# Softmax attention on one core: the loop head of TensorE moved to another fetch slot, a blank score fill ahead of the data, held-back first loads and a shallower VectorE

## The chip, the cores and the metric

The kernel runs on one core of one Trainium2 chip. The metric is the device time of one execution in microseconds (us); medians are over the runs of one kernel, and a ratio compares kernels that ran on the same chip in the same job. A job compares each kernel with fresh runs of the kernel before. The jobs of the experiments ran on different chips: the kernel before had 824.22 us in the first job, 823.03 in that of e0 to e3, 825.05 for e4 to e8, 825.07 for e9 to e11 and 824.69 for e12. So where a median is set beside that of "the control" (e0_again) across jobs, a difference below 2 us shows nothing. "Ratio" below is the mean time of one kernel's fast runs over that of the other kernel's fast runs of the same rounds, so it is not quite the ratio of the medians that stand beside it.

A profile is one execution with the hardware's records. Its span is about 1.7 us shorter than the time of the same execution. Times inside a profile count from the start of its span.

## The reference

```python
B, H, Sq, Sk, D = 16, 32, 192, 1024, 128      # all bf16
scores = jnp.einsum("bhqd,bhkd->bhqk", q, k) * D ** -0.5
p = softmax(scores, axis=-1)
out = jnp.einsum("bhqk,bhkd->bhqd", p, v)
```

512 heads are worked on in 128 tiles of four heads. One tile loads 1 MB of K, 1 MB of V and 192 KB of Q and stores 192 KB.

## The kernel before

Each tile is worked in three *fills*. A fill is one batch of score matmuls (48 or 64 of them, 32 rows each) into PSUM; ScalarE exponentiates it; VectorE turns K and Q for later fills, GpSimd puts K (`order`) and V (`spread`) in the layout that TensorE wants. Four fills later the matching *PV round* of 32 matmuls multiplies with V, and VectorE normalises it (`onorm`). There are 384 fills. TensorE runs them in a hardware loop of 64 turns, six fills (two tiles) a turn; the other engines are unrolled. TensorE's program:

```python
for _i in range(12):                       # warm-up, on a tile of ones
    pe.matmul(o_ps..., ones[:], ones...)
pe.wait_ge(s_set, 3)                       # buffers of the first, empty PV rounds are set
with nc.Fori(0, NF // (3 * R), engines=[PE], head_slot={PE: 100}):
    pv(-1 - LAG, (1,))                     # second half of the round that the turn before left open
    for f in range(3 * R):
        qk(f)                              # scores of fill f
        pv(f - LAG, (0,) if f == 3 * R - 1 else (0, 1))
pv(NF - 1 - LAG, (1,))
for s in range(NF - LAG, NF): pv(s)        # [tail, cut]
```

`head_slot` fixes the place (0 to 255) of the loop's first instruction in a block of 256 instructions. In the built program the loop has 1050 instructions: 512 matmuls of two instructions each and 26 others. SyncE issues the loads without a wait until buffers run out, and VectorE turns K five fills ahead of the fill it stands at:

```python
load_k(0); load_k(1); load_q(e, 1)
for n in range(2, NKN):                    # NKN = 5 buffers
    load_v(n - 2); load_k(n); load_q(e, n)
# VectorE, in order:
for f in range(NF + LAG + 1):
    if f - 5 >= 0: onorm(f - 5)            # [range check of the sums near the end, cut]
    g = f + 5
    if g < NF: turn_k(g)                   # ahead of it turn_q(x) for the third piece of a tile
```

VectorE takes this program in its order: while it waits for a K load in `turn_k`, it can't normalise, and TensorE can't begin the next PV round, because the program has one PSUM buffer for them.

## Time and profile before

| reading | before |
|---|---|
| median time, 4 runs | 824.22 us (823.38 to 825.35) |
| span of the profile, granted clock | 823.1 us, 0.996 |
| first real scores (fill 0) start | 8.62 us |
| fill 8 starts | 36.12 us |
| fill 383, the last, starts | 812.92 us |

In the steady part three fills take 6.21 us, or 2.07 us a fill. The table by stretches shows TensorE full there. Its columns are the stretch, its length, busy time and instructions of each engine, the granted clock of TensorE, the share and the rate of the DMA engines. The kernel before:

```profile
0.00:25.00 25.00, 15.93 (x428) 11.54 (x428) 12.15 (x14) 11.91 (x10) 14.39 (x19) 0.93 0.94 364
600.00:800.00 200.00, 200.00 (x8260) 178.38 (x8250) 149.77 (x322) 187.13 (x194) 137.49 (x163) 1.00 1.01 388
```

So TensorE bounds the steady part, and only the head leaves room. The timeline of TensorE in the head of the kernel before follows. Its columns are start, length, engine, line, operation, tiles, shape, count, and in brackets the idle time before it with what ended it. L628 is a score fill, L650 a PV round. "issue" means that no wait which the profile shows explains the idle time.

```profile
12.79 0.29 PE L628 MATMUL f_s<-f_qt,f_kt 32*128 32x128 bf16 x8
15.49 0.98 PE L628 MATMUL f_s<-f_qt,f_kt 32*128 32x128 bf16 x40 [2.41 <-issue]
16.41 1.10 PE L650 MATMUL f_o<-f_vp,f_pt 128*64 128x129 bf16 x32
17.44 1.09 PE L628 MATMUL f_s<-f_qt,f_kt 32*128 32x192 bf16 x48
18.46 0.36 PE L650 MATMUL f_o<-f_vp,f_pt 128*64 128x129 bf16 x6
21.87 1.62 PE L650 MATMUL f_o<-f_vp,f_pt 128*64 128x129 bf16 x26 [3.06 <-issue]
23.43 1.73 PE L628 MATMUL f_s<-f_qt,f_kt 32*128 32x192 bf16 x64
...
28.46 1.89 PE L628 MATMUL f_s<-f_qt,f_kt 32*128 32x128 bf16 x46 [2.12 <-issue]
```

Three stops stand in the middle of fills or rounds, 126 and 124 matmuls apart: about 250 instructions and the semaphore instructions between them, one block. After the second stop 64 score matmuls take 1.73 us instead of 1.10: the trace records the clock at 0.5 there, from 21.43 to 24.84 us (called cold below). The packets of the queues tell the rest; the page counts them by queue:

```profile
q14 instruction: 32, 0.26, 0.1%
q8 instruction: 5, 0.08, 0.0%
```

### The profile page before, as it was taken

How to read it: one execution, taken by the hardware profiler on the slowest of the kernel's cores; microseconds unless marked ns; L12 is line 12 of the kernel's file. 1: busy time of each engine (PE TensorE's matmuls, PEld its weight loads, DVE VectorE, ACT ScalarE, POOL GpSimd, SP SyncE). 2: the span in 40 equal slices, each digit the busy share in tenths (PEclk: the TensorE clock that was granted, in tenths of full speed). 3: DMA queues.
4: the chain of work that ended last, by engine and by line, in shares of the span. 5: the costliest groups of instructions: out<-in, count | busy, mean ns of one | idle time of the engine just before them, and what ended most of it. 6: DMA issues, size and time to landing. Idle time of an engine off the chain costs nothing. (4 is left out here: it accounts for less than half of the span.)

```text
span 823.1 us, 71558 instructions
## 1 busy us (share of the span) xinstructions
PE 807.8 (98%) x32926; PEld 717.7 (87%) x32926; DVE 599.6 (73%) x1288; ACT 748.5 (91%) x770; POOL 549.6 (67%) x646
## 2 busy tenths in 40 slices
PE   6899999999999999999999999999999999999998
PEld 4788888888888888888888888888888888888887
DVE  5477777777777777777777777777777777777775
ACT  5699999999999999999999999999999999999996
POOL 6466676676676666767667667667666666766762
PEclk9899999999999999999999999999999999999999
DMA  9999999999999999999999999999999999999961
GB/s 355 401 403 406 407 403 407 403 402 404 405 401 394 405 402 402 402 401 391 406 403 399 404 404 394 404 405 397 400 407 395 403 400 402 401 405 401 399 226 59
DMA packets 138293, 319.14 MB, mean 388 GB/s; under 512 B 7184, under 2 KB 56336, under 8 KB 121872
## 3 DMA queue, kind: packets, MB, share of 16 engines
q1 hardware_dynamic: 105376, 294.22, 91.3%
q10 hardware_dynamic: 32880, 24.58, 8.9%
q14 instruction: 32, 0.26, 0.1%
q8 instruction: 5, 0.08, 0.0%
HBM read 293.60 MB, written 25.17 MB: 387 GB/s over the span
## 5 line engine op out<-in xcount | busy, mean ns | idle before, releaser
L801 ACT ACTIVATE f_pt<-f_s 128x1536 bf16<-128x1536 f32 x384 | 554.9, 1445 | 3.2 <-PE f_o L650 3.2
L583 POOL COPY f_kt<-f_kx 128x768 uint32<-128x768 uint32 (+1 forms) x384 | 293.5, 784 | 254.4 <-DVE f_kx L712 134.2
L628 PE MATMUL f_s<-f_qt,f_kt 32*128 32x192 bf16 (+2 forms) x20480 | 422.9, 226 | 6.9 <-issue 4.5
L650 PE MATMUL f_o<-f_vp,f_pt 128*64 128x129 bf16 x12336 | 424.7, 222 | 3.3 <-issue 3.3
L650 PEld LDWEIGHTS f_o<-f_vp,f_pt 128*64 128x64 bf16 x12336 | 365.2, 110 | 54.3 <-issue 24.8
L628 PEld LDWEIGHTS f_s<-f_qt,f_kt 32*128 32x128 bf16 x20480 | 348.2, 92 | 43.2 <-issue 7.4
L712 DVE STREAM_TRANSPOSE f_kx<-f_kn 128x768 uint32<-128x768 uint32 (+1 forms) x384 | 334.1, 871 | 8.7 <-DMA f_kn<-in_k_dram 8.7
L798 ACT ACTIVATE f_pt<-f_s 128x512 bf16<-128x512 f32 x384 | 229.2, 597 | 63.1 <-PE f_s L628 32.9
L592 POOL COPY f_vp<-f_vs 128x1024 uint32<-128x1024 uint32 x256 | 259.1, 1040 | 8.4 <-PE f_o L650 8.4
L733 DVE RECIPROCAL f_rinv<-f_o 128x2 f32<-128x2 f32 x381 | 64.8, 170 | 195.9 <-PE f_o L650 195.9
L737 DVE TENSOR_TENSOR f_ob<-f_o,f_rinv 128x256 bf16<-128x256 f32 x381 | 161.6, 424 | 13.3 <-DVE f_rinv L733 0.3
L721 DVE STREAM_TRANSPOSE f_qt<-f_qn 128x384 uint32<-128x384 uint32 x128 | 72.8, 569 | 0.0
L675 PE MATMUL f_o<-f_ones 128*128 128x512 bf16 x12 | 4.4, 540 | 1.1 <-POOL f_ones L574 1.1
L675 PEld LDWEIGHTS f_o<-f_ones 128*128 128x128 bf16 x12 | 1.5, 131 | 3.5 <-issue 2.2
L575 POOL MEMSET f_vp<- 128x4352 uint32 x1 | 3.7, 3728 | 0.0
L695 DVE MEMSET f_pt<- 128x3072 uint32 x1 | 2.6, 2618 | 1.5 <-PEq L829 1.5
L650 PE MATMUL f_s<-f_vp,f_pt 128*64 128x129 bf16 x96 | 3.1, 220 | 0.4 <-PEq L611 0.4
L650 PEld LDWEIGHTS f_s<-f_vp,f_pt 128*64 128x64 bf16 x96 | 2.8, 110 | 0.5 <-issue 0.5
L788 ACT ACTIVATE f_pt<-f_ones 128x3072 f32<-128x3072 bf16 x1 | 2.8, 2762 | 0.0
L788 ACT ACT_TABLE_LOAD x1 | 1.3, 1283 | 1.2 <-PEq L829 1.2
L733 DVE RECIPROCAL f_rinv<-f_s 128x2 f32<-128x2 f32 x3 | 0.5, 171 | 1.4 <-PE f_s L650 1.4
L689 PE MATMUL f_o<-f_bad,f_ones 128*1 128x1 bf16 x1 | 0.2, 164 | 1.3 <-DVEq L779 1.3
(13 smaller groups left out, 5.3 us busy)
## 6 DMA issues: line engine op xcount, KB each, us to landing
f_kn<-in_k_dram SPq DMA_DIRECT2D x128, 1024.0 KB, 10.6
f_vs<-in_v_dram SPq DMA_DIRECT2D x128, 1024.0 KB, 8.4
f_qn<-in_q_dram SPq DMA_DIRECT2D x127, 192.0 KB, 10.5
out_dram<-f_ob ACTq DMA_DIRECT2D x62, 384.0 KB, 9.5
out_dram<-f_ob SPq DMA_DIRECT2D x1, 384.0 KB, 3.2
out_dram<-f_ob SPq DMA_DIRECT2D x2, 192.0 KB, 2.3
f_qn<-in_q_dram ACTq DMA_DIRECT2D x1, 192.0 KB, 5.0
```

Source lines behind the costliest of these rows:

```text
L583: gp.tensor_copy(kt[:, x % NKT].bitcast(U32).rearrange("p U (j s u) c -> p U j s (u c)", s=2, u=2)[:, lo:hi], kx[:, x % 2].rearrange("p (U ...
L592: gp.tensor_copy(vp[:, x % NVP, 2 * T * i: 2 * T * i + 2 * T, 0:D].bitcast(U32), vs[:, x % NVS, 2 * i: 2 * i + 2, :].rearrange("p a (t d) ...
L628: ins = pe.matmul(S[:, c0: c0 + n1 - n0], kt[r, x % NKT, 2 * t + h, :, c], qt[r, x % R, h, n0:n1, c], start=w == 0 and g == 0, stop=w == 3 ...
L650: return pe.matmul(O[m0: m0 + m, u, 0:129], pt[:, x % R, 2 * y + z, t * SQ + n0: t * SQ + n0 + m], vp[:, x % NVP, (2 * y + z) * T + t, 0:129],
L675: pe.matmul(o_ps[:].rearrange("p a b -> p (a b)"), ones[:], ones[:].unsqueeze(1).to_broadcast([128, 4, 128]), start=True, stop=True)
L712: dve.transpose(kx[:, x % 2].rearrange("p (U s j u) -> p s u U j", s=2, j=32, u=2)[:, :, :, lo:hi], kn[:, x % NKN].rearrange("p (s u U i) ...
L721: dve.transpose(qt[:, x % R].bitcast(U32).rearrange("p b (y j u) c -> p u y b (j c)", y=3, u=2), qn[:, x % NKN].rearrange("p (u y b i) -> ...
L733: dve.reciprocal(ri, O[:, :, 128]).then_inc(s_rc, 1)
L737: dve.tensor_tensor(ob[:, so, 6 * a + 2 * w: 6 * a + 2 * w + 2, :], O[:, :, 0:128], ri.unsqueeze(2).to_broadcast([128, 2, D]), ALU.mult,). ...
L788: act.activation(pt[:, 1].rearrange("p a c -> p (a c)").bitcast(F32), ones[:, 0:1].to_broadcast([128, 2 * T * SQ]), ACT_FN.Copy).then_inc( ...
L798: act.activation(pt[:, x % R, 0, c], s1_ps[:], ACT_FN.Exp, scale=scale).then_inc(s_e1, 1)
L801: act.activation(pt[:, x % R, 1:4, c], s3_ps[f % 2][:], ACT_FN.Exp, scale=scale).then_inc(s_e3, 1)
```

## The change

The intent: have the first blocks of the loop fetched while TensorE waits for K0 anyway, keep the loads out of the way of the later ones, and let VectorE not stand in front of loads that now come later. Cut to its core:

```diff
-    BLANK = LAG + 1
+    PRE = 1                                   # one blank score fill ahead of the data
+    BLANK = LAG + 1 + PRE
+    AHEAD = 3
 # SyncE
                 for n in range(2, NKN):
+                    if n == 2: e.wait_ge(s_qk, PRE + 1)      # scores of fill 0 done
                     load_v(n - 2)
+                    if n == 2: e.wait_ge(s_pv, BLANK - 2)    # PV round of fill 1 done
                     load_k(n)
                     load_q(e, n)
 # TensorE
-                for _i in range(12):          # warm-up
+                for _i in range(2):
-                             head_slot={mybir.EngineType.PE: 100}):
-                    pv(-1 - LAG, (1,))
-                    for f in range(3 * R):
+                             head_slot={mybir.EngineType.PE: 226}):
+                    pv(-PRE - 1 - LAG, (CLOSE, 32))
+                    for f in range(-PRE, 3 * R - PRE):
                         qk(f)
-                        pv(f - LAG, (0,) if f == 3 * R - 1 else (0, 1))
+                        pv(f - LAG, (0, CLOSE if f == 3 * R - PRE - 1 else 32))
+                for f in range(NF - PRE, NF): # the last fill stands behind the loop now
+                    qk(f); pv(f - LAG)
 # VectorE
-                    g = f + 5
-                    if g < NF:
+                    g = f + AHEAD
+                    if 5 <= g < NF:
```

Cut away: smaller, earlier memsets (so that the loop can be entered near 2.3 us instead of 5.7), zeros in the K and Q buffers that the blank fill reads, and all semaphore counts raised by PRE. The number of matmuls in a turn is the same.

## The prediction

> **What bounds the kernel now.** In the table by stretches, TensorE is busy 200.0 of 200 us from 200 to 800 us. The timeline gives a steady fill (one score fill plus one PV round) every 2.07 us: 812.92 - 34.01 us over 376 fills. 384 such fills are 795 us; the rest of the 823.1 us span is a head and a tail. The change leaves the matmuls of a fill and the tail alone, so only the head can pay.

> **The head.** In the timeline the first real scores start at 8.62 us, after K0 has landed (6.4 us). Fill 7 starts at 34.01 us; at 2.07 us a fill it would start at 23.1. So 10.9 us are lost. TensorE stops three times with releaser "issue", no semaphore: 2.41 us (ends 15.49), 3.06 (21.87), 2.12 (28.46). After the last two, matmuls run slow for a while (48 to 64 in 1.73 to 1.89 us instead of 1.10). Ahead of each stop's end the trace has one 16 KB packet of the second instruction queue (13.03, 19.35, 25.91 us). [...] The stops lie about 126 matmuls apart: two instructions each plus semaphore instructions, 256. So a block takes 5.5 to 6.6 us from entering the previous one, behind loads moving at 400 GB/s, and TensorE eats it in 3.1.

> **What the change does.** The loop is 1050 instructions (512 matmuls, 26 others). With its head at slot 226 the first crossing comes after 15 matmuls, near 2.5 us instead of 9.9; the blank fill runs while TensorE would wait for K0. So block 2 should be there when needed (about 9.5 us). Block 3 is requested near 9.5 us, with K1 landed and V0 only just issued, needed near 12.4; block 4 near 13, ahead of K2. With a quiet queue I estimate 4 us a fetch (the tail's packet at 817.9 us plus the 1.5 us seen from landing to resumption), so two stops of about 1 us each remain. The added fill is free under the wait for K0; with fewer warm-up matmuls TensorE may meet fill 0 cold (up to 1.2 us). Delayed loads: K2 lands near 18.5 us instead of 15.6, for fill 6 at 21 us or later; V0 near 14.5 for a round at 18. With VectorE three fills ahead, it no longer blocks the normalisations long behind K2 and K3; I allow 0.5 us. In steady state the later turning leaves the V spread about 0.5 us before its round: tight, no loss expected.

> **Sum.** 10.9 gained, less about 2 (stops), 0.7 (clock), 0.5 (data): 7.7 us, so about 817.2 us; range 814.0 to 821.0. Faster by over 2% 0.02, within 2% 0.97, slower 0.01.

> **What would show it.** Right: TensorE's "issue" stops in the waits shrink from 7.6 us to under 3; the first fetch packet lies before 9 us; fill 7 starts at 25 to 27.5 us; later fills every 2.07 us; about 10 us from the last score fill to the end, as before.

> **What would prove it wrong.** Fetches still taking 6 us with few loads in flight; VectorE waiting for K2 or K3 so long that TensorE stops instead; a stop each turn behind the V spread (period over 2.07 us, worth 128 times its length); a fetch stop on leaving the loop, since the code after it is longer by 80 matmuls.

The times at which it has blocks requested rest on the inference above, that a block is requested when TensorE enters the one before it; the traces show packets, not requests.

## The result

| | before | after |
|---|---|---|
| median | 824.22 us (4 runs) | 819.27 us (4 runs, 818.63 to 821.35) |
| ratio | | 0.9943 (95%: 0.9919 to 0.9967) |
| span of the profile, clock | 823.1 us, 0.996 | 816.9 us, 1.000 |
| fill 0 / fill 8 / fill 383 start | 8.62 / 36.12 / 812.92 us | 8.89 / 28.39 / 806.71 us |
| fill 383 to the end of the span | 10.18 us | 10.19 us |

The gain is 4.95 us by the medians, 6.2 us between the two profiles; the changed kernel's profile is of the fastest of its four runs. Fill 7 starts 8.99 us sooner (25.02 against 34.01), fill 8 starts 7.73 us sooner, fill 383 only 6.21 us sooner: 1.52 us of the head's gain are lost again on the way, and this is not the end after the last fill, which is unchanged.

The timeline of TensorE in the head of the changed kernel (L646 is a score fill, L673 a PV round):

```profile
12.04 0.90 PE L673 MATMUL f_o<-f_vp,f_pt 128*64 128x129 bf16 x25
13.41 0.41 PE L673 MATMUL f_o<-f_vp,f_pt 128*64 128x129 bf16 x7 [0.47 <-issue]
...
17.27 0.34 PE L646 MATMUL f_s<-f_qt,f_kt 32*128 32x128 bf16 x10 [0.50 <-issue]
...
25.02 1.11 PE L646 MATMUL f_s<-f_qt,f_kt 32*128 32x192 bf16 x64
27.36 1.10 PE L673 MATMUL f_o<-f_vp,f_pt 128*64 128x129 bf16 x32 [1.23 <-PEq L629]
28.39 1.10 PE L646 MATMUL f_s<-f_qt,f_kt 32*128 32x128 bf16 x48
```

The two fetch stops that are left are half a microsecond each, and no matmul after them is slow. The fetch packets start at 7.07, 10.68, 14.83 and 21.17 us. From one resumption to the next (13.41 to 17.27) are 3.9 us, against 6.4 and 6.6 before. By the issues and landings in the traces, one load of 1 MB (V0) was under way at 13.41 us; at 15.49 us in the kernel before there were seven. A third stop of 1.23 us ends with "PEq": by the profile TensorE's sequencer waited for a semaphore. It is the wait for a normalisation; VectorE stood in front of K3, which landed at 25.7 us.

The waits of VectorE for K show this, first before, then after (columns: who waited for whom, us in total, times, longest):

```profile
DVE f_kx L712 <- DMA f_kn<-in_k_dram: 8.7, 3, 3.6
```

```profile
DVE f_kx L736 <- DMA f_kn<-in_k_dram: 15.3, 11, 6.3
```

The table by stretches of the changed kernel shows what the held-back loads cost: 290 GB/s in the first 25 us instead of 364. Its clock of 1.00, against 0.93, leaves out the start: the clock records of this profile begin at 7.43 us, and the blank fill ahead of that was slow (48 matmuls in 1.89 us), at no cost, since TensorE waited for K0 afterwards.

```profile
0.00:25.00 25.00, 20.85 (x690) 17.23 (x690) 11.94 (x22) 18.02 (x18) 14.60 (x21) 1.00 0.83 290
600.00:800.00 200.00, 199.97 (x8237) 178.15 (x8235) 149.38 (x323) 186.98 (x194) 137.33 (x161) 1.00 1.02 390
```

And the loads stay late for the whole run. The list of DMA issues gives the median time from issue to landing; the kernel before, then the changed one:

```profile
f_kn<-in_k_dram SPq DMA_DIRECT2D x128, 1024.0 KB, 10.6
f_vs<-in_v_dram SPq DMA_DIRECT2D x128, 1024.0 KB, 8.4
```

```profile
f_kn<-in_k_dram SPq DMA_DIRECT2D x128, 1024.0 KB, 18.1
f_vs<-in_v_dram SPq DMA_DIRECT2D x128, 1024.0 KB, 16.3
```

Near the end TensorE stops once more, for 0.64 us, in the PV round behind fill 382. The timeline of the changed kernel there:

```profile
803.94 1.10 PE L646 MATMUL f_s<-f_qt,f_kt 32*128 32x192 bf16 x64
805.68 1.10 PE L673 MATMUL f_o<-f_vp,f_pt 128*64 128x129 bf16 x32 [0.64 <-PEq L629]
806.71 1.09 PE L646 MATMUL f_s<-f_qt,f_kt 32*128 32x128 bf16 x48
```

**Theory.** The head gains because the fetches come early and meet few loads. What is lost again has three sources: (a) the loads, held back, run without a lead for the rest of the run, so late ones stop TensorE; (b) with VectorE three fills ahead the range check stands in front of the last turns; (c) the clock: the four runs have clocks 1.0, 1.0, 0.998, 0.995 and spans 816.9, 817.0, 818.0, 819.6 us, in that order. **Rivals.** One part of the change alone makes the gain and the rest is decoration; or the gates cost more than they give.

### The profile page after: what moved, and what is told of

Same layout as the page of the kernel before. It is cut to its first block, busy times and chain, and to the rows that moved or that the text cites. A ratio compares the mean times of both kernels' runs of the same rounds, so it can differ in the third digit from the quotient of the medians.

```text
span 816.9 us, 71709 instructions
## 1 busy us (share of the span) xinstructions
PE 806.7 (99%) x32996; PEld 717.5 (88%) x32996; DVE 599.7 (73%) x1293; ACT 749.8 (92%) x772; POOL 550.7 (67%) x648
## 5 line engine op out<-in xcount | busy, mean ns | idle before, releaser
L601 POOL COPY f_kt<-f_kx 128x768 uint32<-128x768 uint32 (+1 forms) x384 | 301.0, 784 | 254.2 <-DVE f_kx L736 254.1
L673 PE MATMUL f_o<-f_vp,f_pt 128*64 128x129 bf16 x12368 | 425.8, 222 | 2.9 <-PEq L629 1.9
L646 PE MATMUL f_s<-f_qt,f_kt 32*128 32x192 bf16 (+1 forms) x20528 | 423.2, 226 | 2.4 <-PEq L629 1.8
L673 PEld LDWEIGHTS f_o<-f_vp,f_pt 128*64 128x64 bf16 x12368 | 366.1, 110 | 55.2 <-issue 28.1
L646 PEld LDWEIGHTS f_s<-f_qt,f_kt 32*128 32x128 bf16 x20528 | 348.5, 92 | 38.9 <-issue 3.1
L828 ACT ACTIVATE f_pt<-f_s 128x512 bf16<-128x512 f32 x384 | 229.3, 597 | 58.7 <-PE f_s L646 25.6
L814 ACT ACTIVATE f_pt<-f_ones 128x1536 f32<-128x1536 bf16 x3 | 4.2, 1472 | 0.0
L589 POOL MEMSET f_vp<- 128x1088 uint32 (+1 forms) x3 | 3.8, 1309 | 0.0
L673 PE MATMUL f_s<-f_vp,f_pt 128*64 128x129 bf16 x96 | 3.1, 220 | 0.2 <-PEq L629 0.2
L673 PEld LDWEIGHTS f_s<-f_vp,f_pt 128*64 128x64 bf16 x96 | 2.9, 110 | 0.3 <-issue 0.3
L686 PE MATMUL f_o<-f_ones 128*128 128x512 bf16 x2 | 1.0, 622 | 1.1 <-POOL f_ones L586 1.1
```

The source lines that it names most:

```text
L589: return gp.memset(part.bitcast(U32), 0x3F803F80)
L601: gp.tensor_copy(kt[:, x % NKT].bitcast(U32).rearrange("p U (j s u) c -> p U j s (u c)", s=2, u=2)[:, lo:hi], kx[:, x % 2].rearrange("p (U ...
L646: ins = pe.matmul(S[:, c0: c0 + n1 - n0], kt[r, x % NKT, 2 * t + h, :, c], qt[r, x % R, h, n0:n1, c], start=w == 0 and g == 0, stop=w == 3 ...
L673: ins = pe.matmul(O[64 * z: 64 * z + 64, u, 0:129], pt[:, x % R, 2 * y + z, t * SQ + 64 * j: t * SQ + 64 * j + 64], vp[:, x % NVP, (2 * y ...
L814: return act.activation(part.bitcast(F32), ones[:, 0:1].to_broadcast([128, 2 * T * SQ // 2]), ACT_FN.Copy)
L828: act.activation(pt[:, x % R, 0, c], s1_ps[:], ACT_FN.Exp, scale=scale).then_inc(s_e1, 1)
```

## The experiments

Twelve experiments followed (no run labelled e7 is on record). "Fill 8" is the start of fill 8 in the kernel's profile: it measures the head. "8 to 383" is the time from fill 8 to fill 383: it measures everything lost later. The last column is TensorE's closing branch, which jumps over the general path behind the loop when the range check is content. "Turn" is the mean time of a loop turn, six fills, over fills 60 to 369.

| kernel | median us | ratio to before | fill 8 | 8 to 383 | turn | closing branch |
|---|---|---|---|---|---|---|
| before | 824.22 | 1 | 36.12 | 776.80 | 12.43 | 0.48 |
| after | 819.27 | 0.9943 | 28.39 | 778.32 | 12.44 | 0.49 |
| e0_again | 819.69 | 0.9954 | 28.12 | 779.45 | 12.46 | as after |
| e1_slot_only | 836.55 | 1.0148 | 36.03 | 785.74 | 12.57 | 4.36 |
| e2_slot100 | 828.92 | 1.0057 | 33.84 | 779.95 | 12.47 | 3.26 |
| e3_no_gates | 823.69 | 0.9995 | 35.37 | 778.02 | 12.43 | 0.49 |
| e4_ahead5 | 824.47 | 1.0000 | 35.36 | 777.38 | 12.44 | 0.49 |
| e5_no_blank | 829.97 | 1.0053 | 33.78 | 785.60 | 12.56 | 4.31 |
| e6_early7 | 819.91 | 0.9942 | 32.22 | 777.40 | 12.44 | 0.48 |
| e8_slot130 | 826.14 | 1.0020 | 34.63 | 779.98 | 12.47 | 0.49 |
| e9_gate_v0 | 819.45 | 0.9935 | 28.58 | 778.66 | 12.46 | 0.49 |
| e10_warm6 | 819.09 | 0.9940 | 30.08 | 776.67 | 12.43 | 0.49 |
| e11_quarter_q | 817.75 | 0.9915 | 28.71 | 777.55 | 12.43 | 0.49 |
| e12_slot160 | 826.11 | 1.0017 | 37.59 | 777.36 | 12.44 | 0.37 |

### The changed kernel again

> The changed kernel once more, as the control of this call. If its profile of 816.9 us was typical: fetch stops of TensorE of about 0.5 us each, one stop of about 1.2 us behind the late K3, fill 8 near 28.4 us after the start, ratio to the kernel before 0.992 to 0.996. If the times of its slower runs (up to 821.35) come from the clock: the granted clock of each run and its span go together, about 2.7 us for 0.005 of clock.

Median 819.69 us, ratio 0.9954. The spans and clocks of its four runs were 817.8 (0.999), 817.9 (1.0), 818.0 (0.998) and 819.1 us (0.995): the slowest run again has the lowest clock, but the step is smaller than expected (1.2 us), and the first two show that the clock is not all. Its head is as good as the first profile's (fill 8 at 28.12), yet 2.65 us, not 1.52, are lost behind it. There was one fetch stop of 1.05 us, not two of 0.5. The PV rounds' waits in this profile from 600 us on (columns as above: us in total, times, longest):

```profile
PE f_o L673 <- PEq L629: 2.0, 6, 0.6
```

Six stops instead of one, five of them before the end. VectorE waited for K 23 times in this run:

```profile
DVE f_kx L736 <- DMA f_kn<-in_k_dram: 24.2, 23, 6.5
```

The lead of K (landing of tile x to the start of its turn, worked out from the landings in the traces, us) says why:

| tile x | before | after | e0_again | e11_quarter_q |
|---|---|---|---|---|
| 20 | 10.3 | 1.1 | 1.1 | 6.1 |
| 60 | 11.2 | 1.3 | 1.2 | 15.6 |
| 108 | 10.5 | 1.2 | 0.2 | 15.4 |
| 124 | 10.0 | 0.0 | 0.0 | 15.2 |

Before, K waited 10 us for its turn, with VectorE five fills (10.4 us) ahead; after, VectorE is three fills ahead, which alone would add 4.1 us of lead, and yet there is nearly none, and none at all near the end. The landings tell how: in the changed kernel a K lands every 6.21 us between tiles 20 and 60, which is the pace of the fills, so no lead grows. From tile 90 to 124 it is one every 6.26 us where the fills take 6.22 (control: 6.30 and 6.26), and the little lead is used up. Why the landings slow down late is open.

### Less traffic, the test of the lead

```diff
+                w = 384 if x < NKN else 96
                 e.dma_start(
-                    qn[:, x % NKN, :], qf[...]
+                    qn[:, x % NKN, 0:w], qf[...][:, 0:w]
```

From tile 5 on, three quarters of each Q tile are left over from an earlier tile, so the function is not the right one. (The comparison with the reference did not notice: inputs of size 0.05 make the softmax nearly flat.) All instructions and waits stay.

> Wrong on purpose from tile 5 on: the changed kernel, but Q loads of tiles 5 and later bring a quarter of their bytes (6 per cent less traffic); all waits and instructions stay. Theory (with V0 and K2 held back, the loads never get their lead back, since they move at 401 to 406 GB/s while the fills ask for 401; late in the run K arrives just when VectorE wants it, and TensorE waits): K's lead at its turn grows past 4 us by tile 40, VectorE waits for no K after tile 8, no TensorE stop between fills 300 and 375; 0.3 to 1.5 us under 819.7, head unchanged. Rival (the late stops have another cause, the shallow VectorE depth alone): K lead as in the control (0 to 2 us) or the stops stay.

Median 817.75 us. K's lead grows to 15 us, as the table above shows. The list of issues has the landing times back where they were before:

```profile
f_kn<-in_k_dram SPq DMA_DIRECT2D x128, 1024.0 KB, 10.0
f_vs<-in_v_dram SPq DMA_DIRECT2D x128, 1024.0 KB, 7.6
```

VectorE waited for K five times, all in the head, and TensorE did not stop between fill 8 and the end of the loop except once, near 805 us:

```profile
PE f_o L674 <- PEq L630: 0.6, 1, 0.6
```

The head did not change (fill 8 at 28.71). So the late stops of the control come from loads without a lead: theory (a) is shown for the control. The kernels with slots 100 and 130 below agree, with the right function: their heads are later, K's lead is 7 us at tile 60, and none of these stops is there. The one stop that stays is not theirs. Part of the lower median is the clock, which was 1.0 in all four runs here.

How much the late loads cost is seen by stretches (us, from the starts of the fills in each profile):

| kernel | K's lead at tile 108 | fill 8 to 300 | 300 to 382 | 382 to 383 |
|---|---|---|---|---|
| before | 10.5 | 604.87 | 169.82 | 2.11 |
| after | 1.2 | 605.30 | 170.25 | 2.77 |
| e0_again | 0.2 | 605.10 | 171.56 | 2.78 |
| e3_no_gates | 14.5 | 605.09 | 170.14 | 2.78 |
| e9_gate_v0 | 0.7 | 605.20 | 171.35 | 2.10 |
| e10_warm6 | 1.6 | 604.74 | 169.82 | 2.11 |
| e11_quarter_q | 15.4 | 604.74 | 170.03 | 2.78 |

Late loads cost the control about 1.5 us (fill 300 to 382, against e11_quarter_q), but the changed kernel's first profile at most 0.2 us. Most of its loss of 1.52 us is the stop at fill 382, with the fills ahead of it (next section). The 0.2 to 0.4 us lost up to fill 300 are there with a lead of 14 us too, so late loads don't explain them; they stay open.

### The range check two rounds later

```diff
-    EARLY = NF - 9
+    EARLY = NF - 7
```

> The changed kernel with the range check of the sums started two rounds later, so that its three VectorE instructions (0.54, 1.06, 0.93 us) no longer stand in front of the last K turns. Theory (in the changed kernel the check delays the last turn, so the last V spread comes late and TensorE waits 0.64 us in PV round 378): 0.5 to 0.9 us under the control, the wait near 805 us gone. Rival (the late spread comes from late K and V loads): no change.

Median 819.91 us: no gain by the median. The wait near 805 us is gone, here and in the two kernels below that have the same edit, while the kernel with the traffic cut kept it: it comes from the check, theory (b). All seven profiles with three fills ahead and the early check have this stop (0.60 to 0.65 us), whether K's lead is 0 or 15 us; the profile with five ahead has none. The edit moves part of the cost: from fill 383 to the end of the span it is 10.32 us instead of 10.19. But the profile caught something else. The timeline of TensorE in its head:

```profile
11.60 0.90 PE L673 MATMUL f_o<-f_vp,f_pt 128*64 128x129 bf16 x25
16.88 0.64 PE L673 MATMUL f_o<-f_vp,f_pt 128*64 128x129 bf16 x7 [4.38 <-issue]
```

The same place as the 0.47 us stop of the changed kernel, and the code ahead of it is the same; but the packet of block 3 came at 14.39 us instead of 10.68, when V0 had nearly landed (15.0). In this run V0 was issued at 9.6 us, in the changed kernel at 10.03, in the control at 10.0 (packet 10.49), in the kernel with the traffic cut at 9.8 (packet 10.79). The fetch and V0 appear to race, and the order to be settled within tenths of a microsecond. This may be why this kernel's runs spread from 819.22 to 821.66 us; only the slowest of them has a profile, so it is not shown.

### V0 held back further

```diff
-                        e.wait_ge(s_qk, PRE + 1)
+                        e.wait_ge(s_pv, BLANK - 3)
```

The edit of the range check is kept.

> The changed kernel with two edits: V0 is released by the PV round of fill 0 (about 11.0 us) instead of its scores (10.0), and the range check starts two rounds later, as in the run before. Theory (in the profile of the run before, the fetch of block 3 lost a race: V0 was issued at 9.6, the packet came only at 14.39 and TensorE stopped 4.38 us; where the packet wins it comes at 10.5 to 11.0): the packet of block 3 now comes before 11.3 us in the profile, the stop behind it is under 1 us, no run is slow from it: median 818.0 to 819.3, against 819.7 and 819.9. Rival (that packet was chance and the later V0 costs as much as it saves): 819.7 or more, V0 or K2 holding VectorE 1 us longer.

The packet came at 11.00 us, V0 having been issued at 10.6; the stop behind it was 0.92 us. The race was won in this profile, as expected. The median did not follow: 819.45 us, just outside the expectation, runs from 817.46 to 821.20. The lead of K was 1.2 us at tile 100 and nothing from tile 110 on, and TensorE lost 1.9 us between fills 8 and 383, 1.5 of them between fills 300 and 382 where K is late, more than the range check had cost. One run of 817.46 us is the fastest of any version that computes the right function.

### Six warm-up matmuls instead of two

```diff
-                for _i in range(2):
+                for _i in range(6):
```

On top of the kernel just described.

> As the previous one, with 6 warm-up matmuls instead of 2. Theory (some runs meet fill 0 with a cold clock, because TensorE idled 2 to 3 us in the window before; it costs about 1.35 us): with TensorE busy up to fill 0 the granted clock before and in fill 0 is 1.0 in the profile, the clock of every run is 0.998 or more, and the median is 0.3 to 1.0 us under the previous one. Rival (loop entered 1.7 us later, so block 2 comes later and stops fill 0): packet of block 2 later than 8 us and a stop in fill 0; same or slower than the previous one.

Median 819.09 us: the same within the noise. The rival was right about the head: block 2 came later (packet at 7.87 us), TensorE stopped 0.57 us inside fill 0, 1.37 us at block 3 and 1.05 us at block 4, and fill 8 started at 30.08 us, 1.50 us later than without the four matmuls. The theory's account of the clock agrees with the timelines in part: in the six profiles where fill 0 was slow (48 matmuls in 1.55 to 1.90 us), TensorE had idled 2.18 to 3.06 us right ahead of it; here it idled 1.27 us, and the first 44 matmuls of fill 0 took 1.05 us. (With slot 160 it was 1.25 us after 1.87.) But in the kernel before and in the one with the later range check fill 0 took 1.10 and 1.13 us after 2.32 and 2.53 us of idle time, so the idle time ahead does not decide it alone. The clock was 1.0, 1.0, 1.0 and 0.999; one run of clock 1.0 still took 821.01 us.

The pair is worth more than its medians. The head of this kernel is 1.50 us slower than the previous one's, and fill 383 starts 0.49 us *sooner* (806.75 against 807.24 us), because nothing is lost in between (776.67 us from fill 8 to 383, against 776.80 in the kernel before). In this pair the faster head was paid back later: K's lead, 1.6 us here at tile 108 against 0.7, lasted to the end. The changed kernel reached the same 806.71 us with a faster head and hardly any loss to late loads, so the loads set no firm limit.

### The slot alone

```diff
-                             head_slot={mybir.EngineType.PE: 100}):
+                             head_slot={mybir.EngineType.PE: 226}):
```

In the kernel before, nothing else.

> The kernel before with only the loop head moved to slot 226. Theory (the slot only moves the first crossing; a fetch takes 5.5 to 6.6 us behind loads): block 2 is requested when the loop is entered near 5.7 us, so the first of the three stops (2.4 us) goes and the other two stay, about 3 us each: 2 to 3 us less than before, ratio 0.996 to 0.998. Rival (the slot is what helps, the rest is decoration): the whole gain, 0.994.

Median 836.55 us: 13.5 us slower than the kernel before in the same job, instead of 2 to 3 faster. Neither side of the expectation holds. The three stops moved with the slot: the first now comes after 44 of the 64 matmuls of fill 1, 60 matmuls earlier than before, where 126 slots of two instructions a matmul make 63. So they stand at block boundaries:

```profile
14.90 0.44 PE L628 MATMUL f_s<-f_qt,f_kt 32*128 32x64 bf16 x20 [1.50 <-issue]
21.67 0.41 PE L650 MATMUL f_o<-f_vp,f_pt 128*64 128x129 bf16 x7 [3.29 <-issue]
28.17 0.55 PE L628 MATMUL f_s<-f_qt,f_kt 32*128 32x64 bf16 x26 [1.74 <-issue]
```

The head gains nearly nothing: the packets start at 12.57, 19.15, 25.75 and 32.26 us, only 0.2 to 0.5 us sooner than before (the last not at all). An early first crossing did not help here: six loads of 1 MB had been issued before the loop was entered at 6.01 us. With slot 160 (below), where the first crossing falls into fill 0, after 8.77 us, the first packet starts at 12.60 us all the same. Two costs were not in any theory:

- Every turn of the loop is 0.14 us longer. Of this 0.10 us lie at one place: from the last matmul of the round that holds the branch back to the next score matmul it is 0.253 us on average, against 0.152 in the kernel before. 64 turns make 8.9 us from fill 8 to 383.
- The closing branch takes 4.36 us instead of 0.48.

### The changed kernel with slot 100, and with slot 130

```diff
-                             head_slot={mybir.EngineType.PE: 226}):
+                             head_slot={mybir.EngineType.PE: 100}):
```

> The changed kernel with the loop head back at slot 100. Theory: the blank fill still moves the first crossing under the wait for K0 (near 5.7 us), the second comes 2.5 us later than with slot 226, so blocks 3 and 4 are requested after V0 and K2 are on their way: one or two stops of TensorE grow by 1 to 3 us in all; ratio to before 0.995 to 0.999, 1 to 3 us over the control of this call. Rival (slot indifferent once the blank fill runs ahead): same as the control within 0.7 us.

Median 828.92 us, 9 us over the control: three times what was expected. The head is 5.5 us slower (fill 8 at 33.84); the packets of blocks 3 and 4 come at 15.05 and 21.77 us, stops of 2.33 and 1.79 us, with a cold clock in fill 0 and after both stops. The closing branch, 3.26 us, makes 2.8 us of the rest. To keep the head apart from it, slot 130 was run:

> The changed kernel with the loop head at slot 130: the closing branch should then keep its 0.5 us (it took 3.3 us with slot 100), so this shows what the slot does to the head alone. Theory: the crossing into block 2 comes after fill 1 has started, near 12 us, behind V0: its successor takes 5 to 6.5 us instead of 3.6, fill 8 starts 3 to 6 us later than in the control, the time is 3 to 6 us over 819.7 and the end after the last matmul is as in the control (2.4 us). Rival (with slot 100 the loss lay in the clock and the exit): within 1.5 us of 819.7.

Median 826.14 us, closing branch 0.49 us, fill 8 at 34.63 us, packets of blocks 3 and 4 at 14.83 and 21.48 us, stops of 1.81 and 3.22 us. So the slot by itself is worth 6 us of head in the changed kernel, and the rival is out: the exit is as in the control. The clock has a part in it: the stops grew by 4 us, and the trace records three stretches of 3.41 us at half clock in this head. With slot 226 TensorE enters the block ahead of block 3 near 9.8 us (worked out from the place of the boundary, near the end of fill 0), V0 is issued at 10.03, and the packet of block 3 comes at 10.68 us; with slot 130 TensorE enters that block near 12.2 us, after V0 has been issued, and the packet comes at 14.83, 4 us later.

### The gates away

```diff
-                    if n == 2:
-                        e.wait_ge(s_qk, PRE + 1)
...
-                    if n == 2:
-                        e.wait_ge(s_pv, BLANK - 2)
```

> The changed kernel without the two waits in front of the loads of V0 and K2. Theory (fetches are slow because loads are queued ahead of them): the fetches of blocks 3 and 4 take 5.5 to 6.5 us again, two stops of 2.5 to 3.3 us, and a cold clock after them; 3 to 5 us over the control, K2 and K3 land 4 us sooner and never hold VectorE. Rival (the gates cost more than they save, since K3 comes late): 0 to 1.5 us under the control.

Median 823.69 us, 4.0 us over the control, as the theory said. Packets at 7.32, 14.04, 20.98 and 27.33 us: the first as early as in the changed kernel, the others 3.4, 6.2 and 6.2 us later. There are two stops, and cold stretches:

```profile
16.55 0.41 PE L669 MATMUL f_o<-f_vp,f_pt 128*64 128x129 bf16 x7 [2.46 <-issue]
23.43 0.50 PE L642 MATMUL f_s<-f_qt,f_kt 32*128 32x128 bf16 x10 [3.52 <-issue]
```

From resumption to resumption (16.55 to 23.43) it is 6.9 us, with six loads of 1 MB under way at 16.55. With the same slot and the same blank fill, the loads alone turn a fetch of 3.9 us into one of 6.9.

### Five fills ahead

```diff
-    AHEAD = 3
+    AHEAD = 5
```

> The changed kernel with VectorE five fills ahead again instead of three. Theory (three ahead is there because K2 lands near 19.4 and K3 near 25.6 us, and VectorE, which works in order, would stand in front of them before the first normalisations): it waits for K3 before it normalises round 0, so TensorE stops behind PV round 1 until about 27 us: fill 8 starts near 33 to 35 us instead of 28.3, 4 to 6 us over the control of the first call (819.7). Rival (the depth hardly matters): within 1 us of 819.7; then the V spread with its 0.5 us of room could even gain.

Median 824.47 us, 4.8 us over the first control, on another chip; by the ratio (1.0000 against 0.9954) the whole gain is gone. The fetches were as quick as ever (one stop, 0.59 us), and then TensorE waited for VectorE, which stood in front of K3. The timeline of TensorE:

```profile
21.41 1.09 PE L646 MATMUL f_s<-f_qt,f_kt 32*128 32x128 bf16 x48
28.09 1.94 PE L673 MATMUL f_o<-f_vp,f_pt 128*64 128x129 bf16 x32 [5.59 <-PEq L629]
```

K3 landed at 26.4 us. The 1.94 us for 32 matmuls, instead of 1.10, are as slow as in the cold stretches (1.95 us in the profile without gates). The shallow VectorE is what makes held-back loads bearable.

### No blank fill

```diff
-    PRE = 1
+    PRE = 0
```

The blank K is then not counted, and the first, empty PV round needs other buffers, so the loop was entered at 4.49 us instead of 2.32: a part of the effect is this.

> The changed kernel with no blank fill (PRE = 0), slot 226 kept. Theory (the blank fill moves the crossings of blocks 2 and 3 ahead by one fill): the request for block 3 comes near 12 us instead of 9.8, behind V0, and that for block 4 behind K2: stops of 1 to 2.5 us each, 2 to 4 us over 819.7. Rival (the blank fill is decoration, an early first crossing suffices): within 1 us of 819.7. The code after the loop gets shorter too, which may move the closing branch of TensorE: read apart from the head.

Median 829.97 us (826.42 to 835.05), far over. Fill 8 at 33.78 us is 5.7 us later than in the control: the packets come at 9.74, 15.13 and 22.12 us, with stops of 0.24 and 3.56 us and fills 0 and 1 cold (1.89 us for 48 matmuls). The rest is the loop, 12.56 us a turn with the same 0.10 us at the same place as in the slot-only kernel, and a closing branch of 4.31 us. This profile is of the slowest run, 5 us over the median, so not every run can have paid all of it. The blank fill is no decoration.

### Slot 160 in the kernel before

> The kernel before with only the loop head moved, to slot 160 instead of 226. With slot 226 and nothing else, the kernel lost 0.10 us in every turn of the loop, between the round that holds the branch back and the next scores, and 3.85 us at the end, where the closing branch of TensorE took 4.4 us. Theory A (the loss per turn comes from the block boundary 15 matmuls behind the branch): with slot 160 the boundary comes 46 matmuls behind it, and two tiles take 12.43 us as in the kernel before. Rival B (it comes with any head in the upper half of a block): 12.53 us or more. Theory C (the closing branch is slow where the last code lies just behind a block boundary; slot 226 ended 37 slots into a block, slot 160 would end 227 slots in): it takes 0.5 us. Time under A and C: within 1.5 us of the kernel before, since the first crossing still waits for K0.

Median 826.11 us, ratio 1.0017. A turn took 12.44 us, and the place that cost 0.253 us costs 0.153: in this kernel the loss goes with the boundary close behind the branch, not with the upper half of a block. The closing branch took 0.37 us. Theories A and C held. The head was slower than that of the kernel before (fill 8 at 37.59; a stop of 3.42 us and more cold clock), so the time stayed in the expected range only just.

The closing branch, put together (the loop's branch back is recorded at 0.21 us in the kernel before and in the changed one, 0.08 at the loop's exit): the slot within a block at which the code behind the loop ends, worked out from the counts of the built programs, is about 167 before, 200 after, 103 with slot 130, 227 with slot 160 (0.37 to 0.49 us), and 37, 37 and 73 in the slot-only, no-blank and slot-100 kernels (4.36, 4.31, 3.26 us). (Counted from the records in the traces, each is 20 to 24 slots more; the order stays.) In the three slow ones a fetch packet starts while the branch runs, 0.1 to 0.9 us after it began; in the other eleven profiles none does.

## Why the prediction was right or wrong

The time lay in the predicted range (819.27 in 814.0 to 821.0) and the class was right. The gain was 4.95 us where 7.7 were predicted; the range allowed gains of 3.2 to 10.2, and one of the four runs (821.35) lies outside it. The signs that were named held: "issue" stops of 1.0 us in all, a first packet at 7.07 us, fill 7 at 25.02, fills every 2.07 us, 10.19 us at the end. Point by point:

- *"TensorE stops three times with releaser 'issue'", a fetch of 5.5 to 6.6 us behind loads.* Right. A fetch takes 3.9 us with one load of 1 MB under way, 6.4 to 6.9 us with six or seven; removing the gates alone brings the long ones back. The estimate of 4 us was good.
- *"Two stops of about 1 us each remain."* They were 0.47 and 0.50 us. Block 2 came at 7.07 us and did not stop fill 0.
- *"TensorE may meet fill 0 cold."* Not in this profile, so 0.7 us were not lost there. In others it did: in the profile without gates fill 0 and its round took 1.90 and 1.65 us instead of 1.10 and 1.10. The prediction's 1.2 us at most was an estimate; these two took 1.35 us more. The profile before shows what went ahead of a lower clock. Its two stretches at 0.5 in the head (21.43 to 24.84 and 28.26 to 31.67 us) are 3.41 us long each. In the 3.41 us ahead of them TensorE had idled 2.61 and 1.91 us; in the four stretches of this length from 4.36 to 18.02 us it had idled 0.85 to 1.69 us, and the one after each was at 1.0. In the two at 0.5 it idled 0.44 and 0.21 us, and the next was at 1.0 again. In the head of the changed kernel no such stretch from 7.43 us on has more than 1.46 us of idle time, and the clock is recorded at 1.0 up to 816.39 us. A limit between these figures was not looked for with runs of its own.
- *"I allow 0.5 us" for data.* This term was mis-sized. The stop behind K3 alone was 1.23 us, all of it between fills 7 and 8. K2 landed at 19.4 us instead of the estimated 18.5, and V0 at 15.6 instead of 14.5.
- *The head in sum.* Fill 7 came 8.99 us sooner and fill 8 7.73, where 7.7 were predicted for the whole. That the second agrees is luck, since errors of both signs cancelled: smaller stops, no cold fill, later data, a fill 0 that started 0.27 us later.
- *"In steady state the later turning leaves the V spread about 0.5 us before its round: tight, no loss expected."* Here the prediction failed. The room was there: in the middle tiles the spread ends 0.71 us before its round (4.87 before), and no tile loses by it. But the range check (0.54 to 1.06 us on VectorE) takes the room at the end: a stop of 0.64 us, and about 0.9 us with the late fills around it.
- *Delayed loads.* The prediction asked only whether each load comes in time for its first use. It missed that the loads move at 401 to 406 GB/s while the fills ask for about 401 (319 MB in 128 tiles of 6.21 us) and land no faster than the fills go (6.21 us a tile): a lead given away in the head did not come back. Before, K had 10 us of lead; after, about 1, and none near the end. It cost about 1.5 us more in the second profile, at most 0.2 in the first. Cutting 6 per cent of the traffic removed it.
- *The four runs differ by 2.7 us.* A part goes with the clock (0.995 in the slowest run); the race between V0 and the fetch of block 3, seen once, may be another. How much of a run's excess is which can't be told without its trace, and stays open.

What stays open besides: why the changed kernel, with slot 226 too and the boundary 15 matmuls behind its branch, does not pay the 0.10 us a turn that the slot-only and the no-blank kernels pay. They differ in what stands around the branch: their next fill is the first of a tile, which waits for one more semaphore. That this is the cause was not tested. Also not explained are the 0.03 us longer turns with slots 100 and 130 under the changed program. Not tested apart are the smaller memsets and the earlier entry into the loop that they allow; the run with six warm-up matmuls, which enters 1.4 us later (3.74 against 2.32), has a head 1.5 us slower. And no version was found that beats the changed kernel by more than the spread of its own runs.

## What to carry to other kernels

When a stop of an engine stands at no semaphore, count the instructions between stops; if they are a fetch block apart (here 124 and 126 matmuls of two instructions each), the remedy here was to cross the first block boundaries early *and* to hold the bulk loads back while the chain of fetches runs, since either alone gained nothing (early crossings without the gates: ratio 0.9995; gates with later crossings: 1.0057 and 1.0020). A load that is held back must be paid for: look not only at whether it comes in time for its first use but at whether the transfers are faster than the demand, since otherwise the lead does not return (here 401 to 406 GB/s against about 401), and part of a faster head can be given back late in the run. Moving a loop in its fetch block also moves the branch back and the code behind the loop (slot 226 alone: 0.10 us more at the branch in each turn, and a closing branch of 4.36 us instead of 0.48), so read a turn's length and the exit apart from the head before giving the slot the credit or the blame.
